# Turning half of the attention weights with VectorE and a round trip through HBM instead of TensorE

## The chip, the cores and the metric

The kernel runs on one core of a Trainium2 chip, in float32 throughout. The metric is the device time of one execution in microseconds; each kernel is run three times or more and the median is quoted. The names of the engines in the profile are PE (TensorE matmul), PEld (the weight loads of TensorE), DVE (VectorE), ACT (ScalarE), POOL (GpSimd) and SP (SyncE, which issues nearly all of the DMAs here).

## The reference, cut to what matters

Two blocks follow each other: attention in which each query keeps only its 32 largest scores, and a block of layer norm and a two-layer perceptron with a residual.

```python
q, k, v: (8, 8, 576, 64)                       # batch, heads, sequence, head size

scores = matmul(q, k^T) / sqrt(64)
kth    = 32nd largest score of each row
scores = where(scores >= kth, scores, -1e9)
attn   = softmax(scores)                       # + 1e-9 in the denominator
x      = matmul(attn, v), heads side by side   # (8, 576, 512)

xn  = (x - mean(x)) / sqrt(var(x) + 1e-6) * g_ln
out = x + relu(xn @ w_ch1) @ w_ch2             # 512 -> 2048 -> 512
```

## The kernel before, where the change touches it

The work is cut into 160 units. A unit is one pair of heads of one batch and either 128 queries (a whole unit, both heads side by side in two tiles) or the last 64 queries (a rest unit, both heads in one tile). Units that share their keys and whose results are multiplied with the values together form a group of one to three units. The program is written as a loop of steps, one unit entering per step, and the engines' instructions are laid down in this order at build time:

- the scores of unit n+1 (PE, copied to the tile `sc` by ACT),
- the search for the 32nd largest score of unit n (DVE: four MAX8 and three MATCH_REPLACE8 for each tile),
- the masking of unit n-1 and the exponentials of unit n-2 (ACT, in the tile `e`),
- the turning of the weights of unit n-2, because the product with the values needs the keys on the partitions:

```python
def turn(u):
    g = u.group
    if g.pt is None:
        g.pt = ptpool.tile([P, 2 * J + 1, GQ], FP32, tag="pt", name="pt")   # one buffer
    q0 = sum(P for x in g.qts if x < u.qt)

    def part(t):                       # t: head of the pair; J = 4 blocks of 128 keys
        ps = turned()                  # a PSUM bank
        for c in range(J):
            nc.tensor.transpose(
                ps[:, c * P : (c + 1) * P], u.e[:, t, c * P + t * R : (c + 1) * P + t * R],
                ident[:],
            )
        # ... (rest unit left out)
            nc.scalar.copy(
                g.pt[:, t * J : (t + 1) * J, q0 : q0 + P],
                ps[:].rearrange("p (c n) -> p c n", n=P),
            )
    # ... last(): the 64 left-over keys of both heads, one more transpose
```

- and, when the last unit of a group is turned, in the step after it the product with the values (`values`, tile `av`), its return to query rows (`place`, tile `xo`), and, when four pairs of heads are done, layer norm (`stats` on DVE and POOL).

The perceptron has no place of its own in the loop. Its matmuls (`hidden`, tile `hps`, and `project`, tile `ops`) wait in a list `todo`, and calls of `fill()` between the parts of a step take some of them out. How many is decided at build time by estimated costs of the step: what VectorE needs minus what TensorE needs for the attention itself, shared over the eight fills of a step. What is left when the loop ends is laid down after it.

```python
def fill(least=0):
    owed[0] = min(owed[0] + share[0], 6.0)
    while todo and (not todo[0][3] or todo[0][3]()):
        if owed[0] < todo[0][1] / 2 and least <= 0:
            break
        least -= 1
        pop()

def slot(n):
    return max(0.0, dve_cost(n) - pe_cost(n)) / SLOTS
```

The rows of a new block (2 or 3 tiles of 128 rows) must be turned on TensorE before its matmuls. That is allowed as soon as the subtraction of the mean has been laid down, in the same step:

```python
[("turn", 0.44, lambda i=i: turn_x(i), lambda i=i: i in self.centred) for i in range(n)]
```

Of the kernel before, what the change touches and what calls it, by code (L numbers as in the profile page):

```python
# [11 lines left out]
FP32 = mybir.dt.float32  # L12
# [8 lines left out]
J = 4  # L21
# [7 lines left out]
def kernel(  # L29
# [36 lines left out]

    nc = tc.nc
    P = nc.NUM_PARTITIONS  # L70
    B, H, S, D = q.shape
# [3 lines left out]
    JP = J * P  # L75
    R = S - JP
# [6 lines left out]
    def pool(name, bufs, **kw):  # L83
        return ctx.enter_context(tc.tile_pool(name=name, bufs=bufs, **kw))
# [19 lines left out]
    opool = pool("o", 2)  # L104
    xtpool = pool("xt", 1)
    hpool = pool("h", NF)
    psps = pool("ps", 5, space=PSUM)
    mmps = pool("mmps", 3, space=PSUM)

# [88 lines left out]
    now = [-1]  # L198
# [32 lines left out]


    todo = []
    share = [0.0]
    owed = [0.0]

    def done(step):
        return step is not None and step < now[0]

    def pop():  # L240
        kind, cost, run, may = todo.pop(0)
        assert not may or may()
        owed[0] -= cost
        run()
# [55 lines left out]
    class Unit:  # L300
        def __init__(self, job, group, qt):
            self.job, self.group, self.qt = job, group, qt
            self.rest = qt == J
            self.tiles = [(0, 1)] if self.rest else [(0,), (1,)]

    class Group:
        def __init__(self, job, qts):
# [78 lines left out]
    def mask(u, t):  # L386
        nc.scalar.activation(  # L387
            u.e[:, t], u.sc[:, t], AF.Prelu, bias=u.thr[:, t, 7:8], scale=-1.0, alpha=SLOPE
        )

    def weigh(u, t):
        g = u.group
        if g.den is None:
            g.den = denpool.tile([P, 2 * J + 1], FP32, tag="den", name="den")
        col = 2 * u.qt + t
        nc.scalar.activation(  # L396
            u.e[:, t], u.e[:, t], AF.Exp, bias=u.bias[:, t : t + 1], scale=-scale / SLOPE,
            accum_out=g.den[:, col : col + 1],
        )
        if u.rest:  # L400
            den = g.den[:, 2 * J : 2 * J + 1]
        elif t == 1 and u is [x for x in g.units if not x.rest][-1]:
            whole = [qt for qt in g.qts if qt < J]
            den = g.den[:, 2 * whole[0] : 2 * whole[-1] + 2]
            g.sums = den
        else:
            return
        nc.scalar.activation(den, den, AF.Copy, bias=DEN_EPS)

    def turn(u):  # L410

        g = u.group
        if g.pt is None:
            g.pt = ptpool.tile([P, 2 * J + 1, GQ], FP32, tag="pt", name="pt")
        q0 = sum(P for x in g.qts if x < u.qt)

        def part(t):
            ps = turned()
# [3 lines that stand above are left out]
                    ident[:],  # L422
                )
            if u.rest:
                nc.scalar.copy(
                    g.pt[:, 0 : 2 * J, q0 : q0 + R].rearrange(
                        "p (h c) n -> p h c n", h=2
                    ),
                    ps[:].rearrange("p (c h n) -> p h c n", h=2, n=R),
                )  # L430
            else:
                nc.scalar.copy(  # L432
                    g.pt[:, t * J : (t + 1) * J, q0 : q0 + P],
                    ps[:].rearrange("p (c n) -> p c n", n=P),
                )

        def last():
            ps = turned()
            if u.rest:
                nc.tensor.transpose(ps[0:R, 0:P], u.e[:, 0, JP:S], ident[:])  # L440
                nc.tensor.transpose(ps[:, P : 2 * P], u.e[:, 0, JP - R : S], ident[:])
                for h in range(2):
                    nc.scalar.copy(  # L443
                        g.pt[h * R : (h + 1) * R, 2 * J, q0 : q0 + R],
                        ps[h * R : (h + 1) * R, h * (P + R) : h * (P + R) + R],
                    )
            else:
                ends = u.e[:].rearrange("p t n -> p (t n)")[:, JP : JP + P]
                nc.tensor.transpose(ps[:, 0:P], ends, ident[:])  # L449
                nc.scalar.copy(g.pt[:, 2 * J, q0 : q0 + P], ps[:, 0:P])  # L450

        return [lambda t=t: part(t) for t in range(len(u.tiles))] + [last]

    xs, xps, rs, oTr, dr = {}, {}, {}, {}, {}

# [12 lines left out]
    def values(g):  # L468
        vb = g.job.v
        av = brief("av")  # L470
        for c in range(J):
            for h in range(2):
                nc.tensor.matmul(  # L473
                    av[h * D : (h + 1) * D, 0 : g.nq],
                    vb[:, h * J + c, :],
                    g.pt[:, h * J + c, 0 : g.nq],
                    start=(c == 0),
                    stop=False,
                )
        nc.tensor.matmul(  # L480
            av[:, 0 : g.nq], g.job.ends[:], g.pt[:, 2 * J, 0 : g.nq],
            start=False, stop=True,
        )
        g.oT = otpool.tile([P, GQ], FP32, tag="oT", name="oT")
        nc.scalar.copy(g.oT[:, 0 : g.nq], av[:, 0 : g.nq])  # L485
# [38 lines left out]
    class Block:  # L524
        def __init__(self, tiles, dsts):
            self.n = len(tiles)
            self.tiles, self.dsts = tiles, dsts
            self.x = {}
            self.mv = None
            self.centred = set()  # L530
            self.ready = False

        def stats(self, i):
            x = self.x[i]
            if self.mv is None:
                self.mv = small.tile([P, J, 2], FP32, tag="mv", name="mv")
                self.rstd = small.tile([P, J], FP32, tag="rstd", name="rstd")
            st = small.tile([P, 6], FP32, tag="st", name="st")
            nc.vector.bn_stats(out=st[:], in_=x)
            nc.vector.bn_aggr(out=self.mv[:, i, :], in_=st[:])  # L540
            nc.gpsimd.tensor_scalar_sub(x, x, self.mv[:, i, 0:1])
            self.centred.add(i)

        def std(self):
            nc.scalar.activation(
# [8 lines left out]
        def items(self):  # L554
# [38 lines left out]
            def project(i, f):  # L593
                if f == 0:
                    ps["o"] = product("ops")
                nc.tensor.matmul(  # L596
                    ps["o"][:],
                    hT[f][:, i * P : (i + 1) * P],
                    w2[:, f, :],
                    start=(f == 0),  # L600
                    stop=(f == NF - 1),
                )
                if f == NF - 1:
                    o = opool.tile([P, DM], FP32, tag="o", name="o")
                    nc.scalar.activation(  # L605
                        o[:], ps["o"][:], AF.Identity,
                        bias=self.mv[:, i, 0:1], scale=self.rstd[:, i : i + 1],
                    )
                    nc.gpsimd.tensor_tensor(o[:], o[:], self.x[i], ALU.add)  # L609
                    for dst, rows in self.dsts[i]:  # L610
                        nc.sync.dma_start(dst, o[rows, :])

            per_row = 1.71e-3
            return (
                [("turn", 0.44, lambda i=i: turn_x(i), lambda i=i: i in self.centred) for i in range(n)],
                [
                    (
                        "hidden",
# [50 lines left out]

    CONVERTING = max(n for n in batches if batches[n]) + 2  # L670
    EARLY = jobs[NHP].first


    full = slice(0, P)
# [33 lines left out]
    def at(i):  # L708
        return units[i] if 0 <= i < N else None
# [4 lines left out]
        last = at(n - 2) if n - 2 < EARLY else at(n - 3) if n - 3 >= EARLY else None  # L714
        return turned, last.group if last and last is last.group.units[-1] else None

    DVE_UNIT, DVE_REST = 10.3, 5.3


    turns = {}  # L720
# [4 lines left out]
    def pe_cost(n):  # L725
        c = 0.0
        if at(n + 1):
            c += 1.25 if at(n + 1).rest else 1.5
        ex, g = after(n)
        if ex:  # L730
            c += 0.67 if ex.rest else 1.0
        if g:
            c += 3.0
        return c

    def dve_cost(n):
        u = at(n)
        return 5.0 if u is None else DVE_REST if u.rest else DVE_UNIT

    def give(n):  # L740
        early = not all(map(done, ready))
# [32 lines left out]
    for n in range(END):  # L774
# [11 lines left out]
        last = ex and ex is ex.group.units[-1]  # L786
        quick = ex.group if last and ex.group.quick else None

        if ex and not early:
            weigh(ex, 0)  # L790
        if nxt:
            scores(nxt)
        if g:
            values(g)
        if u:
            select(u, 0)
        for den in recips.pop(n, []):
            nc.vector.reciprocal(den, den)
        if n == gives_first:
# [9 lines left out]
            weights(n, 0)  # L809
        fill()  # L810
        if ex and len(ex.tiles) > 1 and not early:
            weigh(ex, 1)
        fill()
        if parts:
            parts[0]()
        if ex and ex.rest:
            keep_den(ex)
# [12 lines left out]
            weights(n, 1)  # L830
        fill()
        if mk and not early:
            mask(mk, 0)
        if g:
            place(g)
        if late:
            place_rest(late.job.b, late.job.hp)
        fill(1 if g or late else 0)
        fill()
        if len(parts) > 2:  # L840
            parts[1]()
        if u:
            select(u, 2)
# [10 lines left out]
        if parts:  # L854
            parts[-1]()
        if mk and len(mk.tiles) > 1 and not early:
            mask(mk, 1)
        fill()
        for x in (u if n < EARLY else None, mk if n > EARLY else None):
            if x and x is units[x.job.last]:  # L860
# [17 lines left out]
            r = late.job.b // 2  # L878
            arrived(n, ("r", r), rs[r])
        fill()  # L880
    while todo:
        pop()


# [29 lines left out]
```

## Time and profile before

| | |
|---|---|
| time, median of 3 | 1763.25 us (1762.53 to 1763.5) |
| span of the profiled execution | 1758.8 us |
| PE busy | 1650.1 us, 94% |
| DVE busy | 1499.0 us, 85% |
| ACT busy | 1153.3 us, 66% |
| POOL busy | 285.6 us, 16% |
| DMA | 66.69 MB moved, q1 16.4% of 16 engines' span |

Busy time of PE is the time covered by at least one matmul; matmuls overlap each other, so the distance between the starts of two neighbours is what one of them costs when the array is kept fed. A wait is the idle time of an engine just before an instruction, with the instruction that released it. The weights of the perceptron are 64-bit floats of which the kernel makes float32 ones in its first sixteen steps; in that stretch ACT and POOL have extra work and TensorE has little.

### The profile page before, as it was taken

The page shows a single profiled execution, that of the slowest core. Times are in us where ns is not written, and L with a number is a line of the kernel's source. Part 1 is how long each engine was busy: PE and PEld are TensorE (multiplying, and loading weights), DVE is VectorE, ACT ScalarE, POOL GpSimd, SP SyncE. Part 2 cuts the span into 40 slices and gives each one's busy share as a digit, 9 for nine tenths or more (in the row PEclk, how much of TensorE's full clock was granted, in tenths as well). Part 3 has the DMA queues.
Part 4 walks back from the last instruction along what each step waited for, and adds up shares of the span by engine and source line. Part 5 has one row for each costly group of instructions (what it writes and reads, how often), then busy time and mean ns, then how long its engine had stood idle before and what let it go on. Part 6 is the DMA issues. An engine that isn't in the chain of part 4 may idle for free.

```text
span 1758.8 us, 23377 instructions
## 1 busy us (share of the span) xinstructions
PE 1650.1 (94%) x7401; PEld 1003.4 (57%) x7401; DVE 1499.0 (85%) x3144; ACT 1153.3 (66%) x2894; POOL 285.6 (16%) x513
## 2 busy tenths in 40 slices
PE   4659889899699999999999999999999999999998
PEld 2337457475355575755546666665555757575564
DVE  7988899989989999999999999999999999950000
ACT  7868877576476776767757776687767777671110
POOL 5664510100100101010111010111001010101000
PEclk6669999999899999999999999999999999999999
DMA  7422232002110022002110111112100210000000
GB/s 178 113 91 78 58 61 41 14 20 47 27 28 17 17 49 45 20 20 47 30 38 21 37 37 28 33 21 53 28 20 23 38 34 21 20 20 12 0 18 12
DMA packets 249347, 66.69 MB, mean 38 GB/s; under 512 B 240516, under 2 KB 240520, under 8 KB 249224
## 3 DMA queue, kind: packets, MB, share of 16 engines
q1 hardware_dynamic: 244488, 64.61, 16.4%
q10 hardware_dynamic: 4736, 0.59, 0.3%
q8 instruction: 59, 0.97, 0.2%
q14 instruction: 64, 0.52, 0.1%
HBM read 55.71 MB, written 9.44 MB: 37 GB/s over the span
## 4 chain that ended last, share of the span: by engine, by line
PE 63%; issue 10%; DVE 8%; ACT 4%; POOL 1%; POOLq 0%; DVEq 0%; ACTq 0%
PE hps L579 21%; PE ops L596 19%; PE scps L340 9%; PE av L473 6%; PE tp L420 5%; DVE m L357 4%; DVE wk L362 3%; PE av L480 2%; ACT e L387 1%; PE tp L566 1%; PE xo L512 1%; ACT oT L485 1%; PE tp L449 1%; ACT pt L432 1%; ACT x L489 0%
## 5 line engine op out<-in xcount | busy, mean ns | idle before, releaser
L357 DVE MAX8 m<-wk 128x8 f32<-128x576 f32 x864 | 612.8, 746 | 2.0
L579 PE MATMUL hps<-xT,w 128*128 128x256 f32 (+1 forms) x2048 | 548.6, 412 | 2.6 <-ACT xT L571 1.3
L596 PE MATMUL ops<-w,h 128*128 128x512 f32 x1152 | 542.2, 599 | 0.0
L579 PEld LDWEIGHTS hps<-xT,w 128*128 128x128 f32 x2048 | 374.8, 192 | 107.8 <-issue 18.4
L362 DVE MATCH_REPLACE8 wk<-m,wk 128x576 f32<-128x576 f32 x576 | 423.9, 743 | 0.0
L596 PEld LDWEIGHTS ops<-w,h 128*128 128x128 f32 x1152 | 201.7, 191 | 177.8 <-issue 174.1
L340 PE MATMUL scps<-kT,qT 64*128 64x288 f32 (+3 forms) x1344 | 252.2, 441 | 33.5 <-DVE qT L296 20.1
L321 ACT COPY sc<-scps 128x288 f32<-128x288 f32 x576 | 197.8, 417 | 61.5 <-PE scps L340 48.6
L357 DVE MAX8 m<-sc 128x8 f32<-128x576 f32 x288 | 203.7, 744 | 36.3 <-ACT sc L321 35.5
L340 PEld LDWEIGHTS scps<-kT,qT 64*128 64x128 f32 (+1 forms) x1344 | 137.6, 182 | 157.5 <-issue 51.2
L396 ACT ACTIVATE e<-e,bias 128x576 f32<-128x576 f32 x288 | 226.9, 788 | 0.8
L387 ACT ACTIVATE e<-sc,m 128x576 f32<-128x576 f32 x288 | 225.7, 784 | 1.5 <-DVE m L357 0.8
L420 PEld LDWEIGHTS tp<-ident,e 128*128 128x128 f32 x1152 | 144.5, 145 | 135.6 <-ACT e L396 67.9
L420 PE MATMUL tp<-ident,e 128*128 128x128 f32 x1152 | 182.1, 283 | 38.2 <-ACT e L396 38.0
L362 DVE MATCH_REPLACE8 wk<-m,sc 128x576 f32<-128x576 f32 x288 | 212.0, 743 | 0.0
L591 ACT ACTIVATE h<-hps 128x256 f32<-128x256 f32 (+1 forms) x256 | 105.5, 412 | 140.9 <-PE hps L579 139.3
L432 ACT COPY pt<-tp 128x512 f32<-128x512 f32 x256 | 149.8, 585 | 64.1 <-PE tp L420 62.4
L473 PE MATMUL av<-pt,vb 128*64 128x256 f32 (+2 forms) x1088 | 144.7, 409 | 0.5 <-ACT pt L443 0.5
L383 POOL TENSOR_TENSOR bias<-m,m 128x2 f32<-128x2 f32 (+1 forms) x144 | 28.0, 195 | 628.1 <-DVE m L357 609.7
L473 PEld LDWEIGHTS av<-pt,vb 128*64 128x64 f32 x1088 | 73.3, 141 | 65.3 <-issue 20.9
L609 POOL TENSOR_TENSOR o<-o,x 128x512 f32<-128x512 f32 x32 | 40.7, 1271 | 369.7 <-ACT o L605 369.7
L485 ACT COPY oT<-av 128x256 f32<-128x256 f32 (+2 forms) x68 | 26.3, 387 | 107.1 <-PE av L480 107.1
(67 smaller groups left out, 1026.0 us busy)
## 6 DMA issues: line engine op xcount, KB each, us to landing
vb<-in_v_dram SPq DMA_DIRECT2D x136, 128.0 KB, 2.4
raw<-in_moe_w_ch_dram SPq DMA_DIRECT2D x32, 512.0 KB, 4.2
kin<-in_k_dram SPq DMA_DIRECT2D x128, 72.0 KB, 2.4
qin<-in_q_dram SPq DMA_DIRECT2D x120, 72.0 KB, 2.4
out_dram<-o SPq DMA_DIRECT2D x32, 256.0 KB, 2.1
ends<-in_v_dram SPq DMA_DIRECT2D x136, 16.0 KB, 2.1
dr<-den SPq DMA_DIRECT2D x64, 0.2 KB, 1.7
out_dram<-o SPq DMA_DIRECT2D x8, 128.0 KB, 2.4
```

The costliest lines, as they stand in the source:

```text
L321: nc.scalar.copy(u.sc[:, t, s * HALF : (s + 1) * HALF], made[s][t][:, 0:HALF])
L340: nc.tensor.matmul(ps[i * R : i * R + ql, o : o + width], qT[r, q0 : q0 + ql], kT[r, k0 : k0 + width], start=True, stop=True,)
L357: nc.vector.max(m[:, t, :], u.cur[t])
L362: nc.vector.match_replace(u.wk[t][:], m[:, t, :], u.cur[t], LOWEST)
L387: nc.scalar.activation(u.e[:, t], u.sc[:, t], AF.Prelu, bias=u.thr[:, t, 7:8], scale=-1.0, alpha=SLOPE)
L396: nc.scalar.activation(u.e[:, t], u.e[:, t], AF.Exp, bias=u.bias[:, t : t + 1], scale=-scale / SLOPE, accum_out=g.den[:, col : col + 1],)
L420: nc.tensor.transpose(ps[:, c * P : (c + 1) * P], u.e[:, t, c * P + t * R : (c + 1) * P + t * R], ident[:],)
L432: nc.scalar.copy(g.pt[:, t * J : (t + 1) * J, q0 : q0 + P], ps[:].rearrange("p (c n) -> p c n", n=P),)
L473: nc.tensor.matmul(av[h * D : (h + 1) * D, 0 : g.nq], vb[:, h * J + c, :], g.pt[:, h * J + c, 0 : g.nq], start=(c == 0), stop=False,)
L579: nc.tensor.matmul(ps["h"][:, 0:N], w1[:, c, f * P : (f + 1) * P], xT[0][:, c, 0:N], start=(c == 0), stop=(c == NC - 1),)
L591: nc.scalar.activation(hT[f], ps["h"][:, 0:N], AF.Relu)
L596: nc.tensor.matmul(ps["o"][:], hT[f][:, i * P : (i + 1) * P], w2[:, f, :], start=(f == 0), stop=(f == NF - 1),)
```

## The change

For most whole units the second head's weights are not turned by TensorE any more. VectorE turns them in blocks of 32x32, into the tile that held the unit's scores; a DMA writes this to HBM, and four more read it back so that the blocks land where a full turn would have put them. This is to take work off TensorE and ScalarE (which had to copy the turned weights out of PSUM). The units concerned are the whole units from number 16 on that are not the last of their group: three for each of 4 pairs of heads and 7 batches, 84 in all. The group's tile `pt` keeps its size, but the second head's half of it is now ordered by blocks of 32 queries, and the product with the values and the copies that still go by PSUM follow that order.

Around it some order is changed: for moved units the second head is masked and weighed first and the first head's transposes come later in the step; the rows of a block are turned only a step after their mean was subtracted (but for the first block); stores of the output are issued a step later, behind the DMAs of the moved weights; and the build-time costs that steer `fill()` are set anew.

```diff
+    hbmpool = pool("hbm", 4, space=bass.MemoryType.DRAM)
 ...
+    def move(u):
+        i0 = place_of(u) // 32
+        t = u.sc[:, 1, 0:JP]
+        nc.vector.transpose(
+            t.rearrange("p (j c n) -> p j c n", j=P // 32, c=J),
+            u.e[:, 1, R:S].rearrange("p (c j k) -> p j c k", c=J, k=32),
+        )
+        hbm = hbmpool.tile([P, JP], FP32, tag="turned", name="turned")
+        nc.sync.dma_start(hbm[:], t)
+        for j in range(P // 32):
+            nc.sync.dma_start(
+                u.group.ptB[j * 32 : (j + 1) * 32, i0 : i0 + P // 32].rearrange(
+                    "k i c n -> k i (c n)"
+                ),
+                hbm[:, j * P : (j + 1) * P].rearrange("(i k) x -> k i x", k=32),
+            )
 ...
-        return [lambda t=t: part(t) for t in range(len(u.tiles))] + [last]
+        heads = [0] if u.moved else range(len(u.tiles))
+        return [lambda t=t: part(t) for t in heads] + [last]
 ... in values():
-                    g.pt[:, h * J + c, 0 : g.nq],
+                    g.ptB[:, 0 : g.nq // 32, c, :] if h else g.pt[:, c, 0 : g.nq],
 ... in Block:
-            self.centred.add(i)
+            self.step[i] = now[0]
+        def centred(self, i):
+            return i in self.step and (now[0] <= gives_first or done(self.step[i]))
 ...
-                        nc.sync.dma_start(dst, o[rows, :])
+                        stores.append(lambda d=dst, s=o[rows, :]: nc.sync.dma_start(d, s))
 ...
+    for u in units[CONVERTING:]:
+        u.moved = not u.rest and u is not u.group.units[-1]
 ... the costs that steer fill():
-    DVE_UNIT, DVE_REST = 10.3, 5.3
+    DVE_UNIT, DVE_REST, DVE_MOVE = 10.3, 5.3, 0.8
-            c += 0.67 if ex.rest else 1.0
+            c += 0.67 if ex.rest else 0.55 if ex.moved else 1.0
-            c += 3.0
+            c += 0.6 + 7.8e-3 * g.nq
-        return 5.0 if u is None else DVE_REST if u.rest else DVE_UNIT
+        c = 5.0 if u is None else DVE_REST if u.rest else DVE_UNIT
+        return c + DVE_MOVE if ex and ex.moved else c
 ... in the step:
+        moved = ex is not None and ex.moved
+        order = (1, 0) if moved else (0, 1)
+        sent, stores[:] = stores[:], []
         if ex and not early:
-            weigh(ex, 0)
+            weigh(ex, order[0])
 ...
         if u:
             select(u, 0)
+        if moved:
+            move(ex)
+        for store in sent:
+            store()
 ...
-        if parts:
+        if parts and not moved:
             parts[0]()
 ...
-        if len(parts) > 2:
+        if moved:
+            parts[0]()
+        elif len(parts) > 2:
             parts[1]()
         if u:
             select(u, 2)
```

The small edits that reverse the two masks, count the weighed heads and spread the remaining PSUM copies over the new order are left out here.

More of the change, by code (lines that the diff above doesn't have):

```diff
@@ L233 @@
     todo = []
+    stores = []
     share = [0.0]
@@ L304, in __init__ @@
             self.tiles = [(0, 1)] if self.rest else [(0,), (1,)]
+            self.moved = False
+            self.weighed = 0
     class Group:
@@ L395, in weigh @@
         col = 2 * u.qt + t
+        u.weighed += 1
         nc.scalar.activation(
@@ L401, in weigh @@
             den = g.den[:, 2 * J : 2 * J + 1]
-        elif t == 1 and u is [x for x in g.units if not x.rest][-1]:
+        elif u.weighed == 2 and u is [x for x in g.units if not x.rest][-1]:
             whole = [qt for qt in g.qts if qt < J]
@@ L408, in weigh, with place_of @@
         nc.scalar.activation(den, den, AF.Copy, bias=DEN_EPS)
-    def turn(u):
+    def place_of(u):
         g = u.group
@@ L414, in turn @@
             g.pt = ptpool.tile([P, 2 * J + 1, GQ], FP32, tag="pt", name="pt")
-        q0 = sum(P for x in g.qts if x < u.qt)
+            g.ptB = g.pt[:, J : 2 * J].rearrange("p c n -> p (c n)").rearrange(
+                "p (i c n) -> p i c n", c=J, n=32
+            )
+        return sum(P for x in g.qts if x < u.qt)
+    def move(u):
[13 more added lines that the diff above has]
+                hbm[:, j * P : (j + 1) * P].rearrange("(i k) x -> k i x", k=32),
+            )
+    def turn(u):
+        g = u.group
+        q0 = place_of(u)
+        i0 = q0 // 32
         def part(t):
@@ L424, in part @@
             if u.rest:
+                both = ps[:].rearrange("p (c h n) -> p h c n", h=2, n=R)
+                nc.scalar.copy(g.pt[:, 0:J, q0 : q0 + R], both[:, 0])
                 nc.scalar.copy(
[L426 to L429, printed above, removed]
+                    g.ptB[:, i0 : i0 + R // 32],
+                    both[:, 1].rearrange("p c (i n) -> p i c n", n=32),
+                )
+            elif t == 0:
+                nc.scalar.copy(
+                    g.pt[:, 0:J, q0 : q0 + P], ps[:].rearrange("p (c n) -> p c n", n=P)
                 )
@@ L432, in part @@
                 nc.scalar.copy(
-                    g.pt[:, t * J : (t + 1) * J, q0 : q0 + P],
-                    ps[:].rearrange("p (c n) -> p c n", n=P),
+                    g.ptB[:, i0 : i0 + P // 32],
+                    ps[:].rearrange("p (c i n) -> p i c n", c=J, n=32),
                 )
@@ L529, in __init__ @@
             self.mv = None
-            self.centred = set()
+            self.step = {}
             self.ready = False
@@ L610, in project @@
                     for dst, rows in self.dsts[i]:
-                        nc.sync.dma_start(dst, o[rows, :])
+                        stores.append(lambda d=dst, s=o[rows, :]: nc.sync.dma_start(d, s))
             per_row = 1.71e-3
             return (
-                [("turn", 0.44, lambda i=i: turn_x(i), lambda i=i: i in self.centred) for i in range(n)],
+                [("turn", 0.44, lambda i=i: turn_x(i), lambda i=i: self.centred(i)) for i in range(n)],
                 [
@@ L730, in pe_cost @@
         if ex:
-            c += 0.67 if ex.rest else 1.0
+            c += 0.67 if ex.rest else 0.55 if ex.moved else 1.0
         if g:
-            c += 3.0
+            c += 0.6 + 7.8e-3 * g.nq
         return c
     def dve_cost(n):
-        u = at(n)
-        return 5.0 if u is None else DVE_REST if u.rest else DVE_UNIT
+        u, ex = at(n), after(n)[0]
+        c = 5.0 if u is None else DVE_REST if u.rest else DVE_UNIT
+        return c + DVE_MOVE if ex and ex.moved else c
     def give(n):
@@ L811 @@
         if ex and len(ex.tiles) > 1 and not early:
-            weigh(ex, 1)
+            weigh(ex, order[1])
         fill()
-        if parts:
+        if parts and not moved:
             parts[0]()
@@ L832 @@
         if mk and not early:
-            mask(mk, 0)
+            mask(mk, int(mk.moved))
         if g:
@@ L856 @@
         if mk and len(mk.tiles) > 1 and not early:
-            mask(mk, 1)
+            mask(mk, 1 - int(mk.moved))
         fill()
@@ L880 @@
         fill()
-    while todo:
-        pop()
+    while todo or stores:
+        for store in stores:
+            store()
+        stores.clear()
+        if todo:
+            pop()
 _INS = ['q', 'k', 'v', 'moe_g_ln', 'moe_w_ch1', 'moe_w_ch2']
```

## The prediction

> **What bounds the kernel now.** I read the page's busy rows and its forty slices first, then the busy time by stretches, the groups of instructions, VectorE's waits, and the timeline of one step. The slices (first the page):
>
> ```profile
> PE   4659889899699999999999999999999999999998
> ...
> DVE  7988899989989999999999999999999999950000
> ```
>
> TensorE is at nine tenths or more to the end and VectorE until slice 36. There are two regimes: a loop in which both engines look full, and a tail of pure perceptron work in which VectorE does nothing. By stretches (sum, then busy time of each engine):
>
> ```profile
> 0.00:200.00 200.00, 134.31 (x537) 83.79 (x538) 173.14 (x364) 156.66 (x382) 117.29 (x120) 0.75 0.43 110
> 200.00:600.00 400.00, 368.10 (x1732) 220.62 (x1732) 372.82 (x776) 265.70 (x680) 48.15 (x115) 0.96 0.16 32
> 600.00:1563.00 963.00, 959.29 (x4517) 589.61 (x4514) 951.07 (x2000) 693.63 (x1750) 107.88 (x269) 1.00 0.15 31
> 1563.00:1759.00 196.00, 188.44 (x622) 109.40 (x620) 1.98 (x6) 37.35 (x84) 12.31 (x11) 0.99 0.03 10
> ```
>
> From 600 to 1563 us PE is busy 99.6% and DVE 98.8%. Which of the two sets the pace? VectorE's rows are real work, one instruction after the other. Its waits in the stretches 200 to 300, 300 to 400, 400 to 500, 500 to 600 and 600 to 1563 are put down to the copies of the scores and sum to 4.3 + 6.2 + 9.3 + 5.0 + 7.3 = 32 us; the last of them:
>
> ```profile
> DVE m L357 <- ACT sc L321: 7.3, 6, 2.3
> ```
>
> TensorE's row is elastic. In the timeline of TensorE the same eight score matmuls cover 1.24 us when the array is fed and 2.18 when it is not:
>
> ```profile
> 338.82 2.18 PE L340 MATMUL scps<-kT,qT 64*128 64x288 f32 x8
> ...
> 1004.82 1.24 PE L340 MATMUL scps<-kT,qT 64*128 64x288 f32 x8
> ```
>
> So I counted the matmuls of the program's listing and multiplied them by start-to-start distances of neighbours in the timeline: 0.433 us for each of the two passes of a 512-wide `ops`, 0.217 for a 256-wide and 0.325 for a 384-wide `hps`, 0.109 for a transpose, 1.17 for a unit's scores, 2.4 to 2.9 for a group's product with the values. That gives 1537 us for the whole program, not 1650. For the twenty steps 120 to 139 it gives 178 us of TensorE against 186 of VectorE. TensorE has some 4% of room in the loop; **the loop runs at VectorE's pace, the tail at TensorE's**. The end is: end of VectorE's last search (1563), plus a handover of some 20 us, plus what is left of `todo`.
>
> **What the Trainium skill says.** "Perfetto Trace Analysis", section Identifying the Most-Contended Engine: matmul busy time is a poor measure of how near TensorE is to its limit, while occupancy is a fair one for VectorE. The trace agrees: 1650 us busy against 1537 counted. "VectorE: DVE Perf Modes", section The three transpose paths: VectorE turns 32x32 blocks only, TensorE a full 128x128 into PSUM; hence the detour, since blocks have to change partitions. The microarchitecture reference of the Vector Engine ("Vector Engine (DVE) Microarchitecture Reference", section 3.8 on the reshape front-end) says that the transpose sustains one element per cycle and lane; the trace has the same operation at 736 ns for 576 elements, as dear as a MAX8 of that length (746). "SBUF — State Buffer", section Door 1: The DMA port swizzle, says that access in whole 16-byte lines is at full rate; the second head's half of `pt` is read in runs of 32 floats, so I expect the product with the values to stay as it is. No run here shows that yet.
>
> **Part by part.** The cost rows among the groups of instructions (busy, mean ns of one, idle before), and the timeline of TensorE around one set of transposes:
>
> ```profile
> L432 ACT COPY pt<-tp 128x512 f32<-128x512 f32 x256 | 149.8, 585 | 64.1 <-PE tp L420 62.4
> ...
> L296 DVE STREAM_TRANSPOSE qT<-qin 128x576 f32<-128x576 f32 x32 | 23.6, 736 | 0.0
> ```
>
> ```profile
> 1001.60 0.60 PE L420 MATMUL tp<-ident,e 128*128 128x128 f32 x4
> 1002.03 1.02 PE L596 MATMUL ops<-w,h 128*128 128x512 f32 x2
> ```
>
> 1. TensorE loses 84 x 4 = 336 transposes (the listings have 1344 and 1008 of `e`). Four start at 1001.60 and the next matmul at 1002.03, so four cost 0.43 us, not the 0.60 they cover nor 4 x 273 ns: 84 x 0.43 = 36 us. This is the whole gain if TensorE were the pace everywhere.
> 2. ScalarE loses 84 copies of 585 ns, 49 us. It is 72% busy in the loop and ends no long wait there; worth little by itself.
> 3. VectorE gains 84 transposes of 512 elements. The distance of two neighbours of 576 elements is 0.69 us (456.83 to 457.52); times 512/576 it is 0.61, say 0.62: 84 x 0.62 = 52 us. As VectorE paces the loop, **this lies on the path**: the loop's end moves from 1563 to about 1615.
> 4. What makes up for it is the tail. `fill()` is told of more room per step (0.8 + 0.45 us for a moved unit, and 0.4 us more for a product of 256 queries, 0.1 less for 320), so more perceptron work is laid inside the loop. After the last product with the values the listing of before has 5 `hps` of 256, 112 `ops`, 20 transposes of x or r, 64 `hps` of 384 and 64 of 256; the changed one has 10 of 384, 80 `ops`, 8 transposes and 64 of 256. The difference is 5 x 0.43 + 32 x 0.866 + 54 x 0.65 + 12 x 0.109 = 2.2 + 27.7 + 35.1 + 1.3 = 66 us less tail.
> 5. Turning rows a step later takes waits away: TensorE stood 26 us before block rows for POOL's subtraction (17.8 for x, 8.6 for r), and its scores stood in the queue behind that. 25 of VectorE's 32 us of waits lie before 600 us, several next to such rows (4.3 at 219 us). I book 12 us less.
> 6. New waits: with more filling the twenty steps 120 to 139 have 189 us of TensorE against 193 of VectorE, so the room falls from 4% to 2.4%. In steps 130 to 134 it is 47.2 against 46.0, TensorE over. I book 5 us of waits for the scores.
>
> Sum: 52 - 12 + 5 = 45 us later at the loop's end, 66 us less behind it: 21 us gained. 1763.25 - 21 = **1742 us**.
>
> The DMAs move 84 x 512 KB, 43 MB more, some 28 GB/s over the loop, where DMA is now at 15% share. The way of a moved half is: 0.62 us on DVE, an issue of 0.4, a store landing in 2.1, four issues of 0.5, a load landing in 2.4:
>
> ```profile
> kin<-in_k_dram SPq DMA_DIRECT2D x128, 72.0 KB, 2.4
> ...
> out_dram<-o SPq DMA_DIRECT2D x32, 256.0 KB, 2.1
> ```
>
> That is some 7.5 us from about 3 us into VectorE's step. The product that needs it is laid two steps later at the earliest, some 20 us; TensorE runs up to 7 us ahead of VectorE (scores copied at 1005.6 are first read at 1011.5), which leaves some 4 us. It should be hidden.
>
> **The rivals.** (a) TensorE is the pace everywhere: the gain is step 1's 36 us plus part of the 26 of step 5, 1715 to 1727. For it: 99.6% busy, and the chain of waits has 63% of PE. Against it: the count of 1537, and VectorE at 98.8% with instructions that cannot overlap. (b) The loop runs dry. In the changed listing the list is empty after steps 28 to 30, 40 to 43, 75, 115 and 155, before only after 41 to 43; filled faster, it waits for the next block. TensorE stands idle there (18 us counted for steps 40 to 44 against 51 of VectorE) and then catches up: 49 against 43 in steps 45 to 49. If that holds up the scores, each of some six places costs VectorE 3 to 5 us: 1760 to 1770. (c) The round trip through HBM comes late, or SyncE, which issues in order and now stands before each of these DMAs, delays the loads of k, q and v: a wait of 1 us in each of 68 groups would be 1790 or more. Against it: the 4 us of room. (d) VectorE's new transpose waits for ScalarE's exponential: it is laid first in the step and ScalarE runs ahead, so no.
>
> **Range and chances.** The sure terms are +52 and -66; the loose ones are the waits, from all 32 us gone (1722) to 20 us more (1769). The range is 1724 to 1764. Two per cent faster is below 1728: that needs nearly all waits of VectorE gone, 0.14. Two per cent slower is above 1798 and needs rival (c): 0.03.
>
> **What would show it.** Right: VectorE's transposes of `e` near 0.68 us each and 0.62 apart; VectorE's last search at 1600 to 1620; a tail of some 130 us after it where there were 196; VectorE 97% or more busy from 600 us on while PE's share falls below 99% with holes near steps 40 and 75. Wrong: waits of the `av` matmuls for a DMA, or of VectorE's first MAX8 of a unit for `sc` of more than 35 us in all (rivals b, c), or a loop that ends before 1590 (rival a).

## The result, and the profile after

The changed kernel takes 1752.72 us (median of 4, 1750.65 to 1755.83) against 1762.89 for the kernel before on the same chip: the ratio is 0.9946, 95% interval 0.9925 to 0.9966. It is faster by 10 us, half of what was predicted.

The page's busy row and slices of the changed kernel:

```profile
PE 1624.7 (93%) x7065; PEld 978.2 (56%) x7065; DVE 1547.6 (88%) x3228; ACT 1117.3 (64%) x2842; POOL 287.7 (16%) x513
...
PE   4659999889699999998999999998999999998998
...
DVE  7987999989989999999999999999999999999100
```

VectorE's full stretch reaches one and a half slices further to the right. The busy time by stretches, with the end of VectorE's last search (1627.1) as a border:

```profile
0.00:200.00 200.00, 135.63 (x530) 83.99 (x530) 169.22 (x356) 153.14 (x373) 113.92 (x117) 0.81 0.44 111
200.00:600.00 400.00, 366.14 (x1637) 217.47 (x1638) 378.56 (x786) 254.69 (x670) 51.30 (x116) 0.92 0.23 58
600.00:1627.10 1027.10, 1002.85 (x4502) 608.15 (x4501) 997.09 (x2080) 684.26 (x1743) 112.58 (x272) 0.99 0.24 61
1627.10:1754.00 126.90, 120.06 (x399) 68.60 (x397) 2.75 (x8) 25.18 (x59) 9.86 (x9) 1.00 0.06 17
```

The loop ends at 1627.1 where it ended at 1562.9 (64.2 us later), and behind it lie 126.9 us where there were 195.9 (69.0 less). In the two profiled executions the net is 4.8 us; these two differ by less than the medians do. In the loop VectorE's busy time rose by 47.9 us (the first three stretches sum to 1544.9 against 1497.0), so the loop also holds 16.3 us more of its idle time. The groups of instructions and VectorE's waits from 200 us to the end of the loop (total, times, longest) say where:

```profile
L434 DVE STREAM_TRANSPOSE sc<-e 128x512 f32<-128x512 f32 x84 | 59.2, 705 | 42.5 <-ACT e L404 42.5
```

```profile
DVE sc L434 <- ACT e L404: 40.8, 27, 7.8
DVE m L364 <- ACT sc L328: 4.2, 1, 4.2
```

Before, VectorE waited in that stretch 32.0 us for the scores. Now it waits 4.2 us for them, and 40.8 us in a new place: its transpose of the weights stands for ScalarE's exponential. One such wait, the longest, in the timeline of all engines:

```profile
358.06 9.34 PE L624 MATMUL hps<-xT,w 128*128 128x256 f32 x28 [0.67 <-ACT xT L616]
...
367.24 0.60 PE L457 MATMUL tp<-ident,e 128*128 128x128 f32 x4
...
367.68 4.48 PE L624 MATMUL hps<-xT,w 128*128 128x256 f32 x20
...
372.91 0.77 ACT L394 ACTIVATE e<-sc,m 128x576 f32<-128x576 f32 x1
...
375.84 0.78 ACT L404 ACTIVATE e<-e,bias 128x576 f32<-128x576 f32 x1
...
376.74 0.71 DVE L434 STREAM_TRANSPOSE sc<-e 128x512 f32<-128x512 f32 x1 [7.79 <-ACT e L404]
```

The list of perceptron work was empty just before; the rows of the next block came in, and the fills laid down 14 matmuls at one point (28 instructions, as each float32 matmul here is two passes), then 10 more. ScalarE does its work in the order in which it was laid down, so it takes those results out of PSUM before it reaches the mask (372.91) and the exponential (375.84). VectorE had the rest of its step ready and stood 7.8 us. Two things add to the delay. TensorE came from an idle stretch with a granted clock of 0.50 (358.06 to 362.00; 0.79 from there to 367.24), so the 28 instructions took 9.2 us, 0.33 each, and the 20 after them 0.22 each. And ScalarE loads a function table twice in this step, 1.28 us each time (368.54 and 374.55), for the square root of the layer norm and back for the exponential.

From here on four numbers describe a kernel: its time, the end of the loop (last MAX8 of the search), the time behind it, and VectorE's waits for the exponential and for the scores between 200 us and the end of the loop.

| kernel | time us | loop end | behind | waits |
|---|---|---|---|---|
| before | 1762.9 | 1562.9 | 195.9 | 32.0 |
| changed | 1752.7 | 1627.1 | 126.9 | 45.0 |
| later place of the transpose | 1741.0 | 1608.4 | 129.9 | 29.2 |
| nothing moved, other edits kept | 1754.2 | 1560.5 | 193.9 | 26.3 |
| rows turned in the same step | 1784.3 | 1661.2 | 121.3 | 81.3 |
| moved, but filled as before | 1785.9 | 1590.6 | 193.7 | 13.0 |
| changed, small debt | 1724.4 | 1593.5 | 129.2 | 13.9 |
| changed, small debt and later place | **1720.9** | 1587.2 | 132.0 | 11.2 |
| nothing moved, small debt | 1743.5 | 1542.3 | 198.6 | 9.1 |
| before, small debt | 1760.5 | 1555.2 | 202.2 | 20.6 |
| rows in the same step, small debt | 1768.4 | 1641.0 | 125.0 | 63.1 |
| not turned at all (work left out) | 1735.9 | 1602.0 | 133.5 | 64.3 |
| not turned, small debt (work left out) | 1713.6 | 1577.0 | 136.0 | 45.1 |

### The profile page after: what moved, and what is told of

It is laid out like the page before. It is cut to its first block, busy times and chain, and to the rows that moved or that the text cites. A ratio compares the mean times of both kernels' runs of the same rounds, so it can differ in the third digit from the quotient of the medians.

```text
span 1754.0 us, 23687 instructions
## 1 busy us (share of the span) xinstructions
PE 1624.7 (93%) x7065; PEld 978.2 (56%) x7065; DVE 1547.6 (88%) x3228; ACT 1117.3 (64%) x2842; POOL 287.7 (16%) x513
## 4 chain that ended last, share of the span: by engine, by line
PE 71%; DVE 11%; ACT 8%; issue 7%; POOL 2%; DMA 1%; SPq 0%; POOLq 0%; ACTq 0%; DVEq 0%
PE hps L624 26%; PE ops L641 20%; PE scps L347 9%; PE av L515 7%; DVE m L364 6%; DVE wk L369 5%; PE tp L457 4%; PE av L522 2%; ACT e L404 2%; ACT e L394 1%; PE tp L611 1%; PE xo L554 1%; ACT size L178 1%; PE tp L490 1%; ACT sc L328 1%
## 5 line engine op out<-in xcount | busy, mean ns | idle before, releaser
L641 PE MATMUL ops<-w,h 128*128 128x512 f32 x1152 | 534.6, 598 | 0.0
L624 PEld LDWEIGHTS hps<-xT,w 128*128 128x128 f32 x2048 | 380.8, 194 | 112.8 <-issue 20.1
L347 PE MATMUL scps<-kT,qT 64*128 64x288 f32 (+3 forms) x1344 | 246.5, 446 | 31.4 <-DVE qT L300 14.4
L457 PE MATMUL tp<-ident,e 128*128 128x128 f32 x816 | 134.4, 291 | 44.2 <-ACT e L404 44.0
L457 PEld LDWEIGHTS tp<-ident,e 128*128 128x128 f32 x816 | 104.9, 149 | 119.0 <-ACT e L404 66.7
L390 POOL TENSOR_TENSOR bias<-m,m 128x2 f32<-128x2 f32 (+1 forms) x144 | 28.3, 196 | 833.5 <-DVE m L364 764.5
L515 PE MATMUL av<-pt,vb 128*64 128x256 f32 (+2 forms) x1088 | 150.3, 418 | 3.6 <-DMA vb<-in_v_dram 3.3
L469 ACT COPY pt<-tp 128x512 f32<-128x512 f32 x128 | 75.4, 589 | 57.0 <-PE tp L457 56.5
L527 ACT COPY oT<-av 128x256 f32<-128x256 f32 (+2 forms) x68 | 26.3, 387 | 116.5 <-PE av L522 116.5
L434 DVE STREAM_TRANSPOSE sc<-e 128x512 f32<-128x512 f32 x84 | 59.2, 705 | 42.5 <-ACT e L404 42.5
```

The source lines that it names most:

```text
L347: nc.tensor.matmul(ps[i * R : i * R + ql, o : o + width], qT[r, q0 : q0 + ql], kT[r, k0 : k0 + width], start=True, stop=True,)
L457: nc.tensor.transpose(ps[:, c * P : (c + 1) * P], u.e[:, t, c * P + t * R : (c + 1) * P + t * R], ident[:],)
L469: nc.scalar.copy(g.pt[:, 0:J, q0 : q0 + P], ps[:].rearrange("p (c n) -> p c n", n=P))
L515: nc.tensor.matmul(av[h * D : (h + 1) * D, 0 : g.nq], vb[:, h * J + c, :], g.ptB[:, 0 : g.nq // 32, c, :] if h else g.pt[:, c, 0 : g.nq], ...
L624: nc.tensor.matmul(ps["h"][:, 0:N], w1[:, c, f * P : (f + 1) * P], xT[0][:, c, 0:N], start=(c == 0), stop=(c == NC - 1),)
L641: nc.tensor.matmul(ps["o"][:], hT[f][:, i * P : (i + 1) * P], w2[:, f, :], start=(f == 0), stop=(f == NF - 1),)
```

## The experiments

Theory A: the moves do save time, but the kernel is filled so fast that the list of perceptron work runs dry in several places, and what is then laid down at once to catch up makes ScalarE late for VectorE's new transpose. Rivals: TensorE, filled as it is, is the pace anyway and the wait only shows it (B); the gain came from the side edits and not from the moves (C); the trip through HBM costs.

**The transpose later in the step.** Move and stores go behind the second pass of the search:

```diff
         if u:
             select(u, 0)
-        if moved:
-            move(ex)
-        for store in sent:
-            store()
 ...
             select(u, 1)
+        if moved:
+            move(ex)
+        for store in sent:
+            store()
```

> Only the place of VectorE's transpose is changed: it stands after the unit's second pass of the search instead of after the first, some 2.8 us later in the step. Theory A (the transpose is laid where the exponential of the same step is often not ready, so VectorE stands 42.5 us that it need not stand): its waits for the exponential fall below 20 us, the waits of the first MAX8 for the scores stay below 15 us, and the time falls by 15 to 25 us, to 1728 to 1738. Theory B (TensorE and ScalarE are late after each stretch without perceptron work, and the transpose only shows it first): the wait moves to the scores or to another row and the time stays within 6 us of 1752.

Measured: 1740.98 us, ratio 0.9877 (0.9862 to 0.9892). The waits on the exponential after 200 us fell from 40.8 to 26.3 us and did not come back at the scores (2.9). The direction is that of theory A, but the time is 3 us above its range and the waits on the exponential are not below 20 us (30.7 in the whole run), so the place is only part of the cause.

**Nothing moved.**

```diff
-        u.moved = not u.rest and u is not u.group.units[-1]
+        u.moved = False
```

> No unit is moved; all the other edits stay (rows a step later, stores a step later, the new cost of the product with the values). By the listing its tail is 64 us longer than that of the changed kernel. Theory A (the moves are what gains): 1757 to 1765, near the kernel before, with VectorE's waits in the loop a few us below the 32 of before. If instead the side edits brought the gain (rival C), it is at 1750 or below.

Measured: 1754.18 us, ratio 0.9945 (0.9932 to 0.9957), where the changed kernel has 0.9946. So in the kernel as it stands **the moves, with the fuller filling that is booked for moved units, gain nothing that can be measured, and the side edits all of it**. The time lies between the two ranges, 3 us below that of theory A and 4 above that of rival C; what it says of the kernel as it stands is rival C.

**Rows of a block turned in the same step.**

```diff
-            return i in self.step and (now[0] <= gives_first or done(self.step[i]))
+            return i in self.step
```

> The rows of a block may be turned in the step in which their mean is subtracted, as before; all else as changed. By the listing its tail is 5 us shorter, as the list is dry for a step less. If the delay saves waits as I booked (12 us), the time rises by 5 to 10 us, to 1758 to 1762. If the delay only makes TensorE stand idle a step longer (rival D), the time falls by some 5 us or more, to 1747 or less.

Measured: 1784.26 us, ratio 1.0122 (1.0108 to 1.0136): 32 us slower than the changed kernel, outside both expectations. TensorE's waits from 200 us to the end of the loop, of this kernel:

```profile
PE tp L611 <- POOL r L583: 34.8, 4, 9.3
...
PE tp L611 <- POOL x L583: 18.3, 6, 10.4
```

and of the changed kernel:

```profile
PE tp L611 <- POOL x L583: 10.5, 4, 5.5
PE tp L611 <- POOL r L583: 9.3, 4, 2.6
```

When the list is dry, the rows are the first thing in it; laid in the step of their statistics, TensorE stands before them, and the scores, transposes and exponentials behind stand too. In the kernel before this happened in one place of the loop; with faster filling it happens in five.

**Moved, but filled by the costs of before.**

```diff
-    DVE_UNIT, DVE_REST, DVE_MOVE = 10.3, 5.3, 0.8
+    DVE_UNIT, DVE_REST, DVE_MOVE = 10.3, 5.3, 0.0
-            c += 0.67 if ex.rest else 0.55 if ex.moved else 1.0
+            c += 0.67 if ex.rest else 1.0
-            c += 0.6 + 7.8e-3 * g.nq
+            c += 3.0
```

> Moves and all else as changed, but the filling steered by the costs of before, so that no more perceptron work goes into a step than before. By the listing the tail is 71 us longer than in the changed kernel. If VectorE paces the loop and the shorter tail is what carries the gain (my sum), the loop ends some 10 to 20 us earlier than in the changed kernel, because its waits of 42.5 us on the exponential fall by as much, and the time is 1803 to 1814. If TensorE were the pace everywhere (rival a of the prediction), it is below 1745.

Measured: 1785.92 us, ratio 1.013 (1.0116 to 1.0143), and slower than before: **without the shorter tail the moves lose**. The time is 17 us below my range for the pace of VectorE. The tail is nearly as long as before (193.7 against 195.9) and the loop ends 27.7 us later than before, although VectorE's busy time rose by 47.8: its waits fell to 13.0. Against the changed kernel the tail is 66.8 us longer and the loop 36.5 shorter. So more than half of the perceptron work that the changed kernel laid into the loop came back as a longer loop. I had expected the loop to be 10 to 20 us shorter. TensorE as the pace everywhere is out, since its total work is that of the changed kernel and the time rose by 33 us.

**A cap on the debt of the fills.** After a dry stretch `owed` stands at its cap of 6.0 us. By the bookkeeping of the changed program it stands above 1.2 us with work in the list in nine steps only (13 to 15, 19, 31, 44, 76, 116, 156), all just after a dry or blocked list (blocked: the next work may not be laid down yet). A cap of 1.5 acts there; in all other steps it trims at most 0.07 us.

```diff
-        owed[0] = min(owed[0] + share[0], 6.0)
+        owed[0] = min(owed[0] + share[0], 1.5)
```

> The changed kernel, but the time that the fills may owe is capped at 1.5 us instead of 6.0, so that after a stretch without perceptron work no 6 us of it are laid down at once. By the listing the tail is 4 us longer. Theory A (the catching up after dry stretches makes TensorE and ScalarE late, and VectorE's long waits of 3 to 8 us on the exponential stand just behind it): these long waits go, VectorE's waits in the loop after 200 us fall from 45 to 25 us or less, and the time falls to 1732 to 1742. Rival (the waits come from the tight filling of every step, or from TensorE's lower clock after idling, and not from the catching up): waits of 38 us or more and 1750 to 1758.

Measured: 1724.38 us, ratio to before 0.9786 (0.9772 to 0.9799), 28 us faster than the changed kernel and faster than expected. The same place in its timeline:

```profile
352.03 3.78 PE L624 MATMUL hps<-xT,w 128*128 128x256 f32 x8 [0.68 <-ACT xT L616]
...
355.60 1.06 PE L457 MATMUL tp<-ident,e 128*128 128x128 f32 x4
...
356.46 4.60 PE L624 MATMUL hps<-xT,w 128*128 128x256 f32 x18
...
365.21 0.71 DVE L434 STREAM_TRANSPOSE sc<-e 128x512 f32<-128x512 f32 x1 [2.29 <-ACT e L404]
```

Eight instructions instead of 28 stand before the transposes, and VectorE's wait is 2.3 us instead of 7.8. Its waits on the exponential in the loop are now (total, times, longest):

```profile
DVE sc L434 <- ACT e L404: 13.9, 15, 2.3
```

In all its waits fall from 45.0 to 13.9, the loop ends 33.6 us earlier, and the tail is 2.3 us longer. In the changed kernel the longest wait behind each of the five dry places (7.8, 6.0, 3.8, 3.3 and 3.3 us) made up 24 of the 40.8 us.

Is it the catching up, or the idling and the low clock after it? From 300 to 400 us TensorE idles as much in both kernels (busy 87%) and has the same granted clock (0.88), and the eight instructions at 352.03 run at a clock of 0.50 as the 28 did; what differs there is how much is laid down at that clock ahead of the rest. Elsewhere the cap changes the idling too (the changed kernel, then this one):

```profile
400.00:500.00 100.00, 82.57 (x329) 43.80 (x328) 94.18 (x195) 58.51 (x156) 12.66 (x31) 0.85 0.28 69
```

```profile
400.00:500.00 100.00, 86.74 (x343) 47.04 (x343) 98.33 (x203) 62.40 (x162) 12.02 (x28) 0.88 0.33 78
```

With less laid down at once the list lasts longer, and by the bookkeeping it is no longer empty after steps 115 and 155. How the 28 us divide between the smaller lump and the shorter idling is not shown.

**The cap and the later place together.**

```diff
-        owed[0] = min(owed[0] + share[0], 6.0)
+        owed[0] = min(owed[0] + share[0], 1.5)
 ... and move(ex) with the stores behind select(u, 1)
```

> Both the later place of the transpose (which gave 12 us) and the cap of 1.5 us. If they remove different waits: 1722 to 1732. If they remove the same ones: 1736 to 1742.

Measured: 1720.86 us, ratio 0.9767 (0.9754 to 0.978), the fastest kernel here, 1 us below the range for different waits. But both my ranges rested on a cap worth less than it was: the later place is worth 11.7 us without the cap and 3.5 with it, so the two remove mostly the same waits.

**VectorE's transposes left out.** The DMA takes the weights unturned from `e`; the turning of these weights is left out, all else is laid down as in the changed kernel.

```diff
-        t = u.sc[:, 1, 0:JP]
-        nc.vector.transpose(
-            t.rearrange("p (j c n) -> p j c n", j=P // 32, c=J),
-            u.e[:, 1, R:S].rearrange("p (c j k) -> p j c k", c=J, k=32),
-        )
+        t = u.e[:, 1, R:S]
```

> VectorE's transposes are left out: the DMA takes the second head's weights unturned from their own tile, so the output is not the reference's; everything else, the filling too, is as in the changed kernel. If VectorE's work and its waits both lie on the path, the loop ends 48 + 41 us earlier less some 20 us that come back as waits for the scores: 1680 to 1700. If TensorE, filled as it is, paces the loop as soon as VectorE is that much lighter (20 steps: 188 us counted against 186), it is 1705 to 1730 and the waits for the scores rise above 30 us.

Measured: 1735.89 us, ratio 0.9852 (0.9838 to 0.9865). With 48 us of VectorE's work and all its waits for the exponential before the transpose gone, only 17 us are saved, because the wait turns up at the scores (total, times, longest):

```profile
DVE m L364 <- ACT sc L328: 64.3, 28, 4.3
```

This is rival B's line, and the time lies 6 us above the range given for it: filled like this, TensorE, or ScalarE that copies its scores, sets the pace as soon as VectorE is lighter.

**The trip through HBM made longer.**

```diff
-        nc.sync.dma_start(hbm[:], t)
+        first = hbmpool.tile([P, JP], FP32, tag="first", name="first")
+        nc.sync.dma_start(first[:], t)
+        nc.sync.dma_start(hbm[:], first[:])
```

> The changed kernel with the trip through HBM made longer: the turned half is copied once more from HBM to HBM before it is read back, 21 MB more read and written and some 2.5 us more on the way. If the trip is hidden with some room, as my sum of 4 us says: 1750 to 1756. If it is at its limit, the product with the values waits for the DMA in most of 84 units: 1800 or more.

Measured: 1752.61 us, ratio 0.9949 (0.9935 to 0.9962), the time of the changed kernel. Its DMA issues (packet kind, count, size, median us to landing):

```profile
first<-sc SPq DMA_DIRECT2D x84, 256.0 KB, 2.0
turned<-first SPq DMA_DIRECT2D x84, 256.0 KB, 2.9
pt<-turned SPq DMA_DIRECT2D x336, 64.0 KB, 2.0
```

Another 2.9 us on the way cost nothing: the trip is hidden with room. In neither kernel did a product with the values wait for these DMAs. One product did wait for the load of `v` itself, 3.3 us in the changed kernel and 5.6 here; that is all that came of the fear that the added DMAs delay the other loads.

**Controls for the cap.** The kernel with nothing moved, the kernel before, the one with rows in the same step and the one without turning, each with the cap of 1.5 in place of 6.0 in the same line and no other edit.

> No unit moved, the other edits kept, and the owed time capped at 1.5 us. Against this, the changed kernel with the cap (1724.4) shows what the moves are worth once the catching up is gone. The list of this kernel is dry in only one place of the loop, and its tail is 4 us longer than without the cap. Theory A (the moves do save, and the catching up hid it): 1745 to 1757, so that the moves are worth 20 to 32 us. Rival (the cap itself is the gain, moves or not): 1735 or less.

> The kernel before with the cap of 1.5 us alone. Theory A (only one dry place, 25 us of waits before 600 us of which the cap removes some): 1752 to 1764. If it falls below 1745, the cap would have been worth as much without the change, and the moves little.

> The changed kernel with the cap of 1.5 us, but rows turned in the same step again (which cost 32 us with the cap of 6.0). If the delay matters because TensorE, waiting for POOL's subtraction, holds up the exponentials behind it whatever the cap: 1740 to 1756. If it mattered only together with the catching up: 1720 to 1730.

> VectorE's transposes left out (the output is not the reference's) with the cap of 1.5 us. Without the cap leaving them out gave only 17 us. If VectorE paces the loop now, its 48 us come off nearly whole: 1676 to 1692. If TensorE as filled paces it as soon as VectorE is lighter: 1698 to 1715, with 30 us or more of waits for the scores.

Measured: nothing moved 1743.54 (ratio 0.9891, 0.9876 to 0.9907); before 1760.48 (0.9989, 0.9983 to 0.9996); rows in the same step 1768.36 (1.0033, 1.002 to 1.0045); not turned 1713.64 (0.9723, 0.971 to 0.9736). So the cap is worth 1.9 us in the kernel before, 10.6 with nothing moved and 28.3 in the changed kernel. By the bookkeeping without the cap the list runs dry in one, two and five places of these loops (with nothing moved in steps 29 to 30 and 41 to 43, not in one place only as I had expected): the more often, the more the cap is worth. With the cap the moves, with the filling booked for them, gain 1743.5 - 1724.4 = 19 us, where without it they gain nothing (1743.5 is 1.5 us below the range for theory A and far above the one for its rival). The delay of the rows is worth 44 us with the cap, so it does not depend on the catching up; the time of that kernel, 1768, is 12 us above the higher of my two ranges. And leaving out the turning saves 11 us with the cap, inside the range for TensorE as the pace: VectorE's 48 us and its 13.9 us of waits are then traded for 45.1 us of waits for the scores, so at this filling the two engines are nearly in balance.

## Why the prediction was half right

The range held the result and the direction was right; the size, 21 us, was twice what came (10). By its own steps:

1. *TensorE loses 336 transposes, 36 us; not the pace everywhere.* The count is as predicted and the rival "TensorE is the pace everywhere" fell: filled as before, the same TensorE work ends 33 us later than in the changed kernel.
2. *ScalarE's copies are worth little.* ACT's busy time fell by 36 us, 49 were booked. No run isolates what that was worth.
3. *VectorE gains 52 us on the path.* Busy time rose by 48.6; one transpose is 705 ns and its successor starts 0.63 us later (365.21 to 365.84 in the kernel with the cap). Right, 3 us too high.
4. *66 us less tail.* 69.0 in the traces. Right.
5. *Rows a step later: 12 us less of waits.* The sign was right, the size far off: undoing it costs 32 us in the changed kernel and 44 with the cap. I took it from the waits of the kernel before, where the list was dry in one place; I knew from the listing that the changed one would be dry in five and did not carry that over.
6. *New waits: 5 us.* **This is the step that failed.** Steps 5 and 6 together booked 7 us less idle time of VectorE in the loop; it was 16.3 more, and 64 minus 69 took the place of 45 minus 66. I reckoned TensorE's room as an average over twenty steps (189 us against 193) and called rival (b), the dry list and the catching up, a rival instead of a term of the sum. It was a term: the cap, which limits the catching up and shortens the idling a little, takes 28 us off the changed kernel. Its mechanism was as I described it; the place where it bites was not. So the sign named for it, more than 35 us of waits for the scores, did not show (8.5 us in the whole run): the waits stood at the transpose.
7. *Rival (d): the transpose waits for the exponential; "ScalarE runs ahead, so no".* Wrong. This is where 40.8 of the 45.0 us stand. In the kernel before, what VectorE needed from ScalarE in a step had been made in the step before; the new transpose needs an exponential of its own step, after one pass of the search. The lead in one step (scores copied at 1005.6, first read at 1011.5) was not ScalarE's lead after a dry list. The later place of the transpose gives 11.7 us back; that much hung on the place.
8. *The trip through HBM is hidden.* Right; 2.9 us more are hidden too.

Two sums in the prediction do not come out, and nothing rests on them: with all 32 us of waits gone the time would be 1763 + 52 - 66 - 32 = 1717, not 1722, and 1 us in each of 68 groups on top of 1742 is 1810, not 1790.

My sum does describe the moves once the catching up is gone: with the cap they lengthen the loop by 51 us (1593.5 - 1542.3) and shorten the tail by 69, net 18 in the traces, against 45 and 66 predicted. That the 21 us of the prediction come near these 18 is partly chance, since it counted side edits as well.

What stays open: the side edits were not taken apart in the kernel without moves, so it isn't known how much of its 9.5 us is the delay of the rows, how much the new cost of the product with the values and how much the later stores. And no run fills the kernel without moves as full as the changed one. So the 19 us belong to the moves together with their fuller filling; what fuller filling would give alone is not shown.

## What to carry to other kernels

When work is laid between other work by a budget, the question is not only how much room each step has on average but what the schedule does after the filler has run out: a budget that saves up while there is nothing to lay down pays itself out in one lump, and in-order engines carry that lump to the one that sets the pace. An instruction moved onto a pacing engine should depend on what was finished a step ago, or be placed late in the step. And a change that looks neutral can be a gain that its own schedule gives back: compare the kernels with and without it under a schedule that suits both.

## What the runs showed of the hardware

The block transpose that reads in runs of 32 floats (its source is a four-dimensional pattern) takes about as long as a plain one: 705 ns for 512 elements against 735 for the 576 of q in the same run, and 0.63 us from its start to the next instruction (with the cap) against 0.69 for 576 elements (in the kernel before). Matmuls of which half take their moving operand in runs of 32 floats are no slower: the sixteen of 256 columns cover the same time in the kernel before and in the changed one.

```profile
1005.99 1.95 PE L473 MATMUL av<-pt,vb 128*64 128x256 f32 x16
```

```profile
787.80 1.95 PE L515 MATMUL av<-pt,vb 128*64 128x256 f32 x16
```

Matmuls after an idle stretch were slow at first: in the kernel with the cap the eight instructions from 352.03 on, with 256 columns each, took 0.45 us apiece to the start of the next at 355.60, at a granted clock of 0.50; the eighteen from 356.46 to 360.89 took 0.25 at 0.88.
